# Two more attention scores a phase through VectorE and one exponential over 3072 columns

## The chip, the cores and the metric

The kernel runs on one core of a Trainium2 chip. The metric is the time of one execution on the device, in microseconds (us); smaller is better. Before the change three runs gave 1272.70, 1272.88 and 1272.94, so the median is 1272.88 us.

The engines are called as in the profile: PE is TensorE (PEld its weight loads), DVE is VectorE, ACT is ScalarE, POOL is GpSimd, and SP issues the DMAs.

## What is computed

The reference mixes two results for each of 2048 tokens of 512 channels: a full softmax attention with 32 heads of 16 channels, and a token-mixing MLP, weighted by a gate of each token.

```python
def reference(A_x, A_wqkv, A_wo, B_x, B_w1, B_b1, B_w2, B_b2, gate_w):
    x = A_x                                   # (1, 2048, 512)
    g = sigmoid((x * gate_w).sum(-1, keepdims=True))
    # a: qkv = x @ wqkv; 32 heads of 16; softmax(q k^T / 4) v; then @ wo
    # b: layernorm(x); gelu over tokens with w1 (2048x1792), b1; then w2, b2
    return g * a + (1 - g) * b
```

Everything is float32. For each head there are 2048 x 2048 scores, and every one goes through an exponential on ACT.

## The kernel before

**Stages.** Until about 278 us the kernel projects q, k and v and computes the first MLP layer. Then come 128 *phases* of attention, and at the end the output projection of the last tokens. The second MLP layer, the projections of late queries and those of the first half of the output run as *dense* matmuls inside the phases.

**A phase.** A group `grp` is two heads by 1024 queries; it has four phases (`ph` 0 to 3). A phase computes 16 scores, numbered `n` = 0 to 15, each a matmul into one PSUM bank of 128 x 512 (L1025). Heads take one half of PE's rows each, and a dense matmul (L1034) runs in the other half beside the first `n_b` scores; `n_b` is 14 in phases of the second layer and 12 in those of a projection. Scores get to exponentials by three roads:

- SINGLE, n = 0, 2, 4, 6, 8, 9: ACT reads the bank and writes `p1` (L1046, 128x512).
- TWO, pairs (10,11), (12,13), (14,15): ACT reads two adjacent banks at once and writes `p2` (L991, 128x1024). The helper is `exps(n)`.
- EVAC, n = 1, 3, 5, 7: DVE copies the bank to `pe` in SBUF (L1042), and at the phase's end ACT takes the exponential of all four in place (L1057, 128x2048).

Then PE multiplies the exponentials by v into the bank `av` (L921, the function `apply_v`), and DVE adds `av` to the sums `ot` (L943). What a phase cannot have in time is *held*: its EVAC units (`HELD`) and its last pair are multiplied at the start of the next phase's `apply_v`.

**PSUM.** Eight banks: one is `dn`, the accumulator of the dense matmuls, with one buffer; seven serve scores and `av`. Score 10 takes the bank of score 3, score 11 that of 4, and so on to 14 (bank of 7, which was first that of 0) and 15 (bank of 8); `av` takes that of 9. Each waits until DVE or ACT has read what was there. Score 6 of a phase takes the bank that `av` had in the phase before, and so waits for DVE's addition.

**Order.** The attention part stands under a manual schedule: each engine runs its instructions in the order of the Python code. On DVE a phase is: its copies, then what a finished dense row needs (`second_out` L542, `out` of a late query L604 to L611, `output` L791), a tiny memset `mark`, splits of weights (L67), jobs put there by `on_dve` (L1073), and the additions L943. The late query's `out` reads `dn` in its first three operations and in its last, the `TENSOR_REDUCE` of L611, and the first dense matmul of the next phase writes `dn` anew. There are eight late queries.

**A wait written by hand.** The exponential over the copies waits for DVE's copies; by L1058 it also waits for an ACT instruction, `pairs_done[1]`, the second pair's exponential of the phase. With that on record a later instruction needs to wait for one engine alone:

```python
tc.add_manual_dep(done.ins, pairs_done[1].ins.name, SYNC, reason=EARLY)
```

Of the kernel before, what the change touches and what calls it, by code (L numbers as in the profile page):

```python
# [9 lines left out]
F32 = mybir.dt.float32  # L10
# [13 lines left out]
P = 128  # L24
# [8 lines left out]
NB = 512  # L33
# [27 lines left out]
def gated_mix(ctx: ExitStack, tc: tile.TileContext, a_x, a_wqkv, a_wo, b_w1, b_b1, b_w2, b_b2, gate_w, out):  # L61
# [116 lines left out]
    with tc.tile_pool(name="vp", bufs=1, side="right") as pool:  # L178
# [15 lines left out]
        turns = {}  # L194
# [378 lines left out]
    LAST = NG * PHASES - 1  # L573
# [301 lines left out]

    token, mark = (out_pool.tile([1, 1], F32, name=name, bufs=1) for name in ("token", "mark"))

    EVAC = 1, 3, 5, 7
    SINGLE = 0, 2, 4, 6, 8, 9
    TWO = (10, 11), (12, 13), (14, 15)  # L880
    TURNS = [(0, 2), (4, 6), (8, 9), *TWO]
    HELD = [(1, 3), (5, 7)]

    def shares(n):

# [62 lines left out]
    with tc.manual_schedule(engines=engines):  # L948
        held, fence, turn, spare = [], None, 0, 0
        landed.clear()  # L950

        for p in range(LAST + 1):
            grp, ph = divmod(p, PHASES)
            second = ph % 2
            if ph == 0:
                sums[grp] = ot_pool.tile([P, NB], F32, name="ot")
                latest["clear"] = nc.gpsimd.memset(sums[grp], 0.0)
                at = [[0, 0], [0, 0]]
                if grp + 1 < NG:
                    qt[grp + 1] = load_q(grp + 1)  # L960
            if ph == 1 and grp + 1 < NG:
                kt[grp + 1] = load_k(grp + 1)
            for what, *args in calls.get(p, ()):
                what(*args)
            if not second:
                beside = [step(*args) for step, *args in dense.get(p // 2, ())]
            n_b = len(beside)
            half = slice(0, HALF) if second else slice(HALF, P)

            head = [second if n < n_b else (n - n_b + second * n_b) % 2 for n in range(NSC)]  # L970
            qbs = {}
            order = list(TURNS)
            if ph == 0 and n_b == NSC - 4:
                order[-2:] = (12, 14), (13, 15)
            for a, b in order + HELD:
                if head[a] == head[b]:
                    qbs[a], qbs[b] = 0, 1
                else:
                    zero, one = (a, b) if head[a] == 0 else (b, a)
                    qbs[zero], qbs[one] = turn, 1 - turn  # L980
                    turn = 1 - turn

            swap = ph == PHASES - 1 and p < LAST and n_b == NSC - 2
            if swap:
                order[-2:] = order[:-3:-1]

            def exps(n):
                pt = ptp.tile([P, 2, NB], F32, name="p2", bufs=len(TWO) + 1)
                where = [share[(j - BANKS) % BANKS] for j in (n - 1, n)]
                low = min(where)  # L990
                pairs_done.append(nc.scalar.activation(pt, twos[low, low + 1], AF.Exp, scale=SCALE))  # L991
                for j, k in zip((n - 1, n), where):
                    units[j] = *units[j][:3], pt[:, k - low, :]

            pairs_done = []
            evac = evp.tile([P, len(EVAC), NB], F32, name="pe")
            units = {}
            share = shares(spare)
            pool = regions()
            psum = pool.__enter__()  # L1000
            ones = [psum.tile([P, NB], F32, name=f"s{n}") for n in range(BANKS)]
            for n in range(NSC):
                i, qb = head[n], qbs[n]
                c = at[i][qb]
                at[i][qb] += 1
                if n < TWO[0][0]:
                    if n >= BANKS:
                        ones[share[n - BANKS]] = psum.tile([P, NB], F32, name=f"s{share[n - BANKS]}")
                    s = ones[share[n % BANKS]]
                else:  # L1010
                    if n == TWO[0][0]:
                        pool.__exit__(None, None, None)
                        pool = regions()
                        psum = pool.__enter__()
                        twos = {}
                        for low in range(BANKS):
                            if low == share[2]:
                                av = psum.tile([P, NB], F32, name="av")
                            elif low not in twos:
                                two = psum.tile([P, 2, NB], F32, name=f"t{low}")  # L1020
                                twos[low], twos[low + 1] = two[:, 0, :], two[:, 1, :]
                                twos[low, low + 1] = two
                    s = twos[share[(n - BANKS) % BANKS]]
                rows_i = slice(i * HALF, i * HALF + ROWS)
                nc.tensor.matmul(  # L1025
                    s,
                    kt[grp][rows_i, c * P : (c + 1) * P],
                    qt[grp][rows_i, qb * NB : (qb + 1) * NB],
                    start=True,
                    stop=True,  # L1030
                )
                if n < n_b:
                    ps, a, b, begin, last, done = beside[n]
                    mm = nc.tensor.matmul(ps, a[half], b[half], start=begin and not second, stop=last and bool(second))  # L1034
                    if n == 0 and fence is not None:
                        tc.add_manual_dep(mm.ins, fence.ins.name, SYNC, reason=REASON)
                    if n == n_b - 1:
                        fence = nc.gpsimd.memset(token, 0.0)  # L1038
                        tc.add_manual_dep(fence.ins, mm.ins.name, SYNC, reason=REASON)
                if n in EVAC:  # L1040
                    pt = evac[:, EVAC.index(n), :]
                    nc.vector.tensor_copy(pt, s)  # L1042
                    units[n] = i, c, qb, pt
                elif n in SINGLE:
                    pt = ptp.tile([P, NB], F32, name="p1", bufs=len(SINGLE))
                    nc.scalar.activation(pt, s, AF.Exp, scale=SCALE)  # L1046
                    units[n] = i, c, qb, pt
                else:
                    units[n] = i, c, qb, None
                    if n == TWO[0][1] or n == TWO[1][1] and not swap:  # L1050
                        exps(n)
                    elif n == TWO[2][1]:
                        exps(n)
                        if swap:
                            exps(TWO[1][1])
            for x in ([evac] if p < LAST else [evac[:, :2, :], evac[:, 2:, :]]):
                done = nc.scalar.activation(x, x, AF.Exp, scale=SCALE)  # L1057
            tc.add_manual_dep(done.ins, pairs_done[1].ins.name, SYNC, reason=EARLY)  # L1058
            evac_done.append(done)
            if n_b and second and beside[-1][-1]:  # L1060
                beside[-1][-1]()
            if p == 0:
                shift_rows(nc.gpsimd, k_bufs[1])
            if p:
                met = nc.vector.memset(mark, 0.0)
                for before in (evac_done[-2], latest["add"], latest["clear"]):
                    tc.add_manual_dep(met.ins, before.ins.name, SYNC, reason=EARLY)
            if second:
                for _ in range(2):
                    if len(ready) < 2:  # L1070
                        split_weight(nc.vector.tensor_copy)
            for what, *args in later.get(p, ()):
                what(*args)  # L1073

            turns, now_held = ([tuple(units[n] for n in pair) for pair in pairs] for pairs in (order, HELD))
            spare = share[2]
            if p < LAST:
                now_held = now_held + turns[-1:]
                turns = turns[:-1]
            if ph == 0:  # L1080
                if held:
                    apply_v(av, grp - 1, held, final=True)
                    spare = share[3]
                    av = twos[spare]
                apply_v(av, grp, turns)
            elif p < LAST:
                apply_v(av, grp, held + turns, await_loads=ph == PHASES - 1)
            else:
                ot = sums[grp]
                nc.vector.tensor_scalar_max(ot, ot, least[0])  # L1090
                apply_v(av, grp, held + turns + now_held, final=True)
                last_ot = ot
            pool.__exit__(None, None, None)
            held = now_held
            if ph == PHASES - 1:
                assert at == [[NS, NS], [NS, NS]]
# [166 lines left out]
```

## Time and profile before

| what | value |
|---|---|
| median of the runs | 1272.88 us |
| the profiled execution | 1273.23 us, of which the span of the profile is 1271.4 us |
| granted TensorE clock | 0.999 |
| PE / ACT / DVE / POOL busy over the span | 99% / 85% / 54% / 16% |
| L1046, six singles a phase | 768 exponentials |
| L991, three pairs a phase | 384 exponentials |
| L1057, one over the copies a phase | 129 exponentials (two in the last phase) |
| L1042, four copies a phase | 512 copies |

In the profile's rows of a timeline the columns are start (us from the span's start), duration (us), engine, line and operation, written tile and read tile with their shapes, and how many were merged in the row. A merged row runs from the start of its first instruction to the end of its last. Instructions of ACT overlap: the next one starts before the one ahead of it has ended, so the sum of durations is more than the time that they take.

### The profile page before, as it was taken

The numbers are of one execution on the slowest core, as the hardware profiler recorded it, in microseconds if no ns is written. First come the engines' busy times: TensorE is split into PE (matmuls) and PEld (weight loads), VectorE is DVE, ScalarE is ACT, GpSimd is POOL, SyncE is SP. The second block draws the span as 40 slices with busy tenths as digits, with TensorE's granted clock in tenths as the row PEclk, the third lists the DMA queues.
The fourth block names the chain that finished last, engine by engine and source line by source line (L and its number), as shares of the span: only waits on it lengthen the run. The fifth ranks groups of instructions, "written<-read, shape, count | busy, mean of one in ns | idle before, by whom it ended". The sixth has DMA issues, their size and how long they took to land.

```text
span 1271.4 us, 32690 instructions
## 1 busy us (share of the span) xinstructions
PE 1263.2 (99%) x13342; PEld 827.5 (65%) x13342; DVE 685.1 (54%) x1282; ACT 1076.4 (85%) x1533; POOL 198.9 (16%) x316
## 2 busy tenths in 40 slices
PE   9999999999999999999999999999999999999998
PEld 7888888875666666666566666666666666655556
DVE  5675453176645554555555455554555455456763
ACT  4443343269999999999999999999999999999990
POOL 0220444561011101010110101111111111000000
PEclk9999999999999999999999999999999999999999
DMA  3798443253654443534344443443543443366511
GB/s 132 247 343 328 139 128 100 79 133 114 206 124 102 86 104 77 163 79 97 80 99 101 92 100 74 90 86 77 116 101 63 98 100 60 56 167 184 140 57 70
DMA packets 100555, 152.32 MB, mean 120 GB/s; under 512 B 17109, under 2 KB 56171, under 8 KB 96300
## 3 DMA queue, kind: packets, MB, share of 16 engines
q1 hardware_dynamic: 99820, 149.08, 45.6%
q8 instruction: 108, 1.77, 0.6%
q10 hardware_dynamic: 576, 1.05, 0.2%
q14 instruction: 51, 0.42, 0.1%
HBM read 105.39 MB, written 44.68 MB: 118 GB/s over the span
## 4 chain that ended last, share of the span: by engine, by line
PE 93%; ACT 5%; DMA 0%; DVE 0%; issue 0%; SPq 0%
PE av L921 29%; PE s L1025 21%; PE acc L424 12%; PE t L1025 12%; PE acc L75 8%; PE t L921 5%; PE dn L1034 2%; ACT p L1046 2%; PE pa L1115 2%; ACT p L991 2%; ACT pe L1057 1%; PE acc L199 1%; PE acc L268 0%; DMA x<-in_A_x_dram 0%; PE pa L1145 0%
## 5 line engine op out<-in xcount | busy, mean ns | idle before, releaser
L1046 ACT ACTIVATE p<-s 128x512 f32<-128x512 f32 x768 | 421.8, 863 | 0.1
L991 ACT ACTIVATE p<-t 128x1024 f32<-128x1024 f32 x384 | 404.9, 1341 | 0.0
L1025 PE MATMUL s<-qs,ks 64*128 64x512 f32 x1280 | 329.7, 400 | 0.5 <-ACT p L1046 0.4
L1042 DVE COPY pe<-s 128x512 f32<-128x512 f32 x512 | 318.1, 684 | 4.8 <-PE s L1025 0.6
L921 PE MATMUL av<-p,v 128*32 128x256 f32 x4904 | 288.1, 379 | 0.0
L1025 PEld LDWEIGHTS s<-qs,ks 64*128 64x128 f32 x1280 | 226.1, 184 | 93.5 <-issue 51.9
L1057 ACT ACTIVATE pe<-pe 128x2048 f32<-128x2048 f32 x129 | 286.2, 2222 | 0.0
L943 DVE TENSOR_TENSOR ot<-av,ot 128x512 f32<-128x512 f32 (+2 forms) x140 | 84.8, 606 | 358.0 <-PE av L921 357.7
L921 PEld LDWEIGHTS av<-p,v 128*32 128x32 f32 x4904 | 159.4, 110 | 105.2 <-issue 0.2
L1025 PE MATMUL t<-qs,ks 64*128 64x512 f32 x768 | 189.4, 428 | 0.0
L1034 PE MATMUL dn<-u_hi,w_hi 64*128 64x512 f32 x448 | 182.4, 407 | 0.0
L1034 PE MATMUL dn<-u_lo,w_hi 64*128 64x512 f32 x448 | 182.2, 407 | 0.0
L1034 PE MATMUL dn<-u_hi,w_lo 64*128 64x512 f32 x448 | 182.2, 407 | 0.0
L68 POOL TENSOR_TENSOR w_lo<-w_raw,w_hi 128x512 fp32r<-128x512 f32 (+1 forms) x128 | 152.9, 1201 | 121.4 <-ACT w_hi L67 99.8
L1025 PEld LDWEIGHTS t<-qs,ks 64*128 64x128 f32 x768 | 96.3, 184 | 87.6 <-ACT p L1046 87.5
L1038 POOL MEMSET token<- 1x1 f32 x128 | 12.0, 94 | 829.5 <-PE dn L1034 776.8
L921 PE MATMUL av<-pe,v 128*32 128x256 f32 x2048 | 137.3, 385 | 0.1
L67 ACT CAST w_hi<-w_raw 128x512 fp32r<-128x512 f32 (+1 forms) x67 | 38.0, 570 | 82.7 <-PE acc L424 63.1
L921 PEld LDWEIGHTS av<-pe,v 128*32 128x32 f32 x2048 | 53.5, 109 | 60.9 <-ACT p L1046 38.4
L424 PE MATMUL acc<-h_hi,w_hi 128*128 128x512 f32 x224 | 87.9, 392 | 0.0
L424 PE MATMUL acc<-h_hi,w_lo 128*128 128x512 f32 x224 | 87.8, 392 | 0.0
L424 PE MATMUL acc<-h_lo,w_hi 128*128 128x512 f32 x224 | 87.8, 392 | 0.0
(161 smaller groups left out, 1446.4 us busy)
## 6 DMA issues: line engine op xcount, KB each, us to landing
w_raw<-in_B_w_dram SPq DMA_DIRECT2D x96, 256.0 KB
ks<-kp SPq DMA_DIRECT2D x192, 128.0 KB
qs<-qp SPq DMA_DIRECT2D x256, 64.0 KB
kp<-pc SPq DMA_DIRECT2D x16, 512.0 KB
qp<-pc SPq DMA_DIRECT2D x8, 768.0 KB
qp<-row SPq DMA_DIRECT2D x24, 256.0 KB
v<-v SPq DMA_DIRECT2D x4, 1088.0 KB
x<-in_A_x_dram SPq DMA_DIRECT2D x16, 256.0 KB
```

The costliest lines, as they stand in the source:

```text
L67: copy(hi, src)
L68: return sub(lo, src, hi.bitcast(F32), ALU.subtract)
L75: nc.tensor.matmul(ps, a, b, start=start and n == 0, stop=stop and n == last)
L424: nc.tensor.matmul(p, a, b, start=first and k == 0, stop=last and k == 2)
L921: mm = nc.tensor.matmul(av[32 * j : 32 * (j + 1), i * QC : (i + 1) * QC], vb[b][:, v_at : v_at + 32], pt[:, h * QC : (h + 1) * QC], start= ...
L943: latest["add"] = nc.vector.tensor_tensor(x, y, x, ALU.add)
L991: pairs_done.append(nc.scalar.activation(pt, twos[low, low + 1], AF.Exp, scale=SCALE))
L1025: nc.tensor.matmul(s, kt[grp][rows_i, c * P : (c + 1) * P], qt[grp][rows_i, qb * NB : (qb + 1) * NB], start=True, stop=True,)
L1034: mm = nc.tensor.matmul(ps, a[half], b[half], start=begin and not second, stop=last and bool(second))
L1042: nc.vector.tensor_copy(pt, s)
L1046: nc.scalar.activation(pt, s, AF.Exp, scale=SCALE)
L1057: done = nc.scalar.activation(x, x, AF.Exp, scale=SCALE)
```

## The change

Scores 14 and 15 leave the pairs and join the scores that DVE copies. So DVE makes six copies a phase, ACT has two pairs (10,11) and (12,13), and the exponential over the copies has 3072 columns. `HELD` gets the pair (14,15), so the same two scores are multiplied by v in the next phase as in most phases before. `p2` has two buffers instead of four, `pe` is 3072 wide instead of 2048. Three special orders of the pairs (`order[-2:]`, `swap`) are gone. The order in which PE computes the last scores is made by the list `in_turn`; with n_b = 12 it is 12, 14, 13, 15. The line of the wait by hand is as it was, but `pairs_done` now has two entries.

```diff
-    EVAC = 1, 3, 5, 7
+    EVAC = 1, 3, 5, 7, 14, 15
     SINGLE = 0, 2, 4, 6, 8, 9
-    TWO = (10, 11), (12, 13), (14, 15)
+    TWO = (10, 11), (12, 13)
     TURNS = [(0, 2), (4, 6), (8, 9), *TWO]
-    HELD = [(1, 3), (5, 7)]
+    HELD = [(1, 3), (5, 7), (14, 15)]
...
-            head = [second if n < n_b else (n - n_b + second * n_b) % 2 for n in range(NSC)]
+            alone = NSC - (NSC - n_b) // 2
+            head = [second if n < alone else 1 - second for n in range(NSC)]
+            in_turn = list(range(n_b)) + [n for pair in zip(range(n_b, alone), range(alone, NSC)) for n in pair]
             qbs = {}
-            order = list(TURNS)
-            if ph == 0 and n_b == NSC - 4:
-                order[-2:] = (12, 14), (13, 15)
-            for a, b in order + HELD:
+            for a, b in TURNS + HELD:
...
-            swap = ph == PHASES - 1 and p < LAST and n_b == NSC - 2
-            if swap:
-                order[-2:] = order[:-3:-1]
-
             def exps(n):
-                pt = ptp.tile([P, 2, NB], F32, name="p2", bufs=len(TWO) + 1)
+                pt = ptp.tile([P, 2, NB], F32, name="p2", bufs=len(TWO))
...
-            for n in range(NSC):
+            for n in in_turn:
...
-                    if n == TWO[0][1] or n == TWO[1][1] and not swap:
+                    if n in (TWO[0][1], TWO[1][1]):
                         exps(n)
-                    elif n == TWO[2][1]:
-                        exps(n)
-                        if swap:
-                            exps(TWO[1][1])
             for x in ([evac] if p < LAST else [evac[:, :2, :], evac[:, 2:, :]]):
                 done = nc.scalar.activation(x, x, AF.Exp, scale=SCALE)
             tc.add_manual_dep(done.ins, pairs_done[1].ins.name, SYNC, reason=EARLY)
...
-            turns, now_held = ([tuple(units[n] for n in pair) for pair in pairs] for pairs in (order, HELD))
+            turns, now_held = ([tuple(units[n] for n in pair) for pair in pairs] for pairs in (TURNS, HELD))
             spare = share[2]
-            if p < LAST:
-                now_held = now_held + turns[-1:]
-                turns = turns[:-1]
```

On ACT the end of a phase stood so before; `p` is the tile of singles (128x512) and pairs (128x1024), `pe` that of the copies, and the square brackets name the engines whose semaphores are waited for:

```order
L1046 ACTIVATE p_3413<-s_3410 128x512 [waits PE_49]
L991 ACTIVATE p_3428<-t_3422 128x1024 [waits PE_49]
L991 ACTIVATE p_3432<-t_3419 128x1024 [waits PE_49]
L991 ACTIVATE p_3436<-t_3421 128x1024 [waits PE_49]
L1057 ACTIVATE pe<-pe 128x2048 [waits DVE_49,Activation_49]
L1046 ACTIVATE p_3488<-s_3482 128x512 [waits PE_49]
```

And now:

```order
L1041 ACTIVATE p_3414<-s_3411 128x512 [waits PE_49]
L986 ACTIVATE p_3429<-t_3423 128x1024 [waits PE_49]
L986 ACTIVATE p_3435<-t_3420 128x1024 [waits PE_49]
L1048 ACTIVATE pe<-pe 128x3072 [waits DVE_49,Activation_49]
L1041 ACTIVATE p_3489<-s_3483 128x512 [waits PE_49]
```

The third pair is gone. The second pair, for which the exponential over the copies waits on ACT's own semaphore, stood two places ahead of it and now stands directly ahead.

On DVE a phase that ends a late query stood so before; `row` and `z` are what `out` writes, `dn` is the accumulator:

```order
L1042 COPY pe<-s_3511 128x512
L67 CAST row<-dn 128x512
L68 TENSOR_TENSOR row<-dn,row 128x512
L609 TENSOR_SCALAR row<-dn,most 128x512
L610 SCALAR_TENSOR_TENSOR row<-row 128x512
L611 TENSOR_REDUCE z<-dn 128x1
L1065 MEMSET mark 1x1
L943 TENSOR_TENSOR ot<-av,ot 128x512
```

And now:

```order
L1037 COPY pe<-s_3512 128x512
L1037 COPY pe<-t_3532 128x512 x2
L67 CAST row<-dn 128x512
L68 TENSOR_TENSOR row<-dn,row 128x512
L609 TENSOR_SCALAR row<-dn,most 128x512
L610 SCALAR_TENSOR_TENSOR row<-row 128x512
L611 TENSOR_REDUCE z<-dn 128x1
L1056 MEMSET mark 1x1
L943 TENSOR_TENSOR ot<-av,ot 128x512
```

The two copies of the last scores stand between the four early copies and all of DVE's other work of the phase.

## The prediction

> **What bounds the kernel now.** I read the page first, then ACT's timeline, then one phase on all engines.
>
> ```profile
> PE 1263.2 (99%) x13342; PEld 827.5 (65%) x13342; DVE 685.1 (54%) x1282; ACT 1076.4 (85%) x1533; POOL 198.9 (16%) x316
> PE 93%; ACT 5%; DMA 0%; DVE 0%; issue 0%; SPq 0%
> ```
>
> The busy shares and the chain both name PE. But PE's busy time is modelled, and the chain goes back along PE wherever its records touch. The question is who sets the length of a phase, and ACT's timeline tells it: an undisturbed phase, then a disturbed one, then the last.
>
> ```profile
> 711.49 2.25 ACT L1057 ACTIVATE pe<-pe 128x2048 f32<-128x2048 f32 x1
> 713.38 3.31 ACT L1046 ACTIVATE p<-s 128x512 f32<-128x512 f32 x6
> 716.26 3.17 ACT L991 ACTIVATE p<-t 128x1024 f32<-128x1024 f32 x3
> 718.97 2.25 ACT L1057 ACTIVATE pe<-pe 128x2048 f32<-128x2048 f32 x1
> ...
> 1187.48 3.17 ACT L991 ACTIVATE p<-t 128x1024 f32<-128x1024 f32 x3
> 1190.41 2.04 ACT L1057 ACTIVATE pe<-pe 128x2048 f32<-128x2048 f32 x1
> 1192.21 3.17 ACT L1046 ACTIVATE p<-s 128x512 f32<-128x512 f32 x6
> 1195.08 3.06 ACT L991 ACTIVATE p<-t 128x1024 f32<-128x1024 f32 x3
> 1197.79 2.13 ACT L1057 ACTIVATE pe<-pe 128x2048 f32<-128x2048 f32 x1
> ...
> 1232.38 3.15 ACT L991 ACTIVATE p<-t 128x1024 f32<-128x1024 f32 x3
> 1235.09 2.31 ACT L1057 ACTIVATE pe<-pe 128x1024 f32<-128x1024 f32 x2
> ```
>
> From 713.38 to 1192.21 lie 64 phases: 7.48 us each, whether 14 or 12 dense matmuls run beside. So PE's own work does not set the length. Read ends instead of starts. The exponential over the copies ends at 713.74, the sixth single at 716.69 (0.49 each), the third pair at 719.43 (0.91 each), the next one over copies at 721.22 (1.79). These sum to 7.48 with no gap. In the disturbed phase the start of L1057 slips by about 0.2, to 0.24 before the last pair ends (1190.65), and its end (1192.45) and the next (1199.92) still keep 7.48. So **ACT is saturated**, and it stays so because the next instruction has already started when one ends: a start that is a little late costs nothing as long as it comes before that end.
>
> How much earlier is needed is seen in the first phase, where ACT had been idle:
>
> ```profile
> 278.60 3.26 ACT L1046 ACTIVATE p<-s 128x512 f32<-128x512 f32 x6
> 281.70 2.90 ACT L991 ACTIVATE p<-t 128x1024 f32<-128x1024 f32 x3
> 284.42 1.99 ACT L1057 ACTIVATE pe<-pe 128x2048 f32<-128x2048 f32 x1
> 286.22 3.12 ACT L1046 ACTIVATE p<-s 128x512 f32<-128x512 f32 x6
> ```
>
> Starts follow each other by 0.48 for a single (716.26 - 713.38 over 6), 0.905 for a pair (284.42 - 281.70 over 3) and 1.80 after the 2048 columns. Without a queue a pair lasts 2.90 - 2 x 0.905 = 1.09 from start to end, so 0.18 of it lies under the next instruction; queued it lasts 1.36.
>
> **The change on ACT.** If saturation stays, ACT saves one instruction's fixed part. The last phase has 1024 columns from SBUF twice: from the pairs' end (1235.53) to 1237.40, 0.935 each. Another 1024 columns cost 1.79 - 0.935 = 0.855, so 3072 take 2.645 where a pair and 2048 took 0.91 + 1.79 = 2.70: 0.06 a phase, 7.6 us over 127 phases.
>
> But the exponential over the copies waits by hand for `pairs_done[1]`. Before, this was the second of three pairs; a third lay between, and it had ended (719.43 - 0.91 = 718.52) before L1057 started at 718.97, so the wait cost nothing. Now it is the pair directly ahead: **ACT must stand still from the end of that pair until its own semaphore has come back.** The trace before shows no ACT instruction that waits for the one ahead of it. The nearest row is DVE's own chain in the fence below: L67 ends at 454.97, and L68, which reads its result, starts at 455.01, 0.04 later. I take 0.04. Bounds: nothing at all (saturation stays, -0.06 a phase) and 0.15, several times the row.
>
> The new phase, from the first single's start: six singles 6 x 0.478 = 2.87; the first pair 0.905; the second pair, with no queue now, ends 1.08 after its start (a hundredth under the third's 1.09); wait 0.04; from the start of 3072 columns to the next start 1.80 + 0.85 = 2.65 (512 columns more are 0.905 - 0.478 = 0.427). Sum 7.545 against 7.48: **+0.065 a phase, 127 phases, +8.3 us**. By the bounds -7.6 to +22.
>
> The Trainium skill's page "ScalarE: Activation LUTs", section "What ACT_TABLE_LOAD costs", gives an ACTIVATE with immediate operands 186 ns + 0.833 ns a column, and an overlap of about 93 ns between two back to back. By it the stop would cost 0.09 + 0.04, an estimate of 7.42 + 0.13 = 7.55 a phase; its 1.04 for a pair is near the 1.09 of the first phase.
>
> **The change on DVE.** One phase with n_b = 14:
>
> ```profile
> 705.36 0.49 PE L1025 MATMUL s<-qs,ks 64*128 64x512 f32 x1
> 705.89 3.31 ACT L1046 ACTIVATE p<-s 128x512 f32<-128x512 f32 x6
> 706.12 2.48 DVE L1042 COPY pe<-s 128x512 f32<-128x512 f32 x4
> 708.84 0.42 PE L1025 MATMUL t<-qs,ks 64*128 64x512 f32 x2
> 709.25 1.07 PE L921 MATMUL av<-pe,v 128*32 128x256 f32 x16
> 712.98 0.69 DVE L943 TENSOR_TENSOR ot<-av,ot 128x512 f32<-128x512 f32 x1 [3.83 <-PE av L921]
> ```
>
> Copies follow each other by (2.48 - 0.69)/3 = 0.60. Scores 14 and 15 end at 709.26; their copies run from 709.29 to 710.58, while the second pair ends at about 711.03 (709.20 for the last single, plus 2 x 0.91). So the copies are in time by 0.4 and do not set L1057. The two copies themselves (2 x 0.60 x 128 phases = 154 us of DVE) are hidden in DVE's idle time. The price is that everything behind them starts about 4.43 after the first copy instead of 2.41, and must be done when the addition is due, 6.86 after it. This window of 2.4 to 2.5 us is enough for most phases, and not for two kinds.
>
> *Late queries, 8 phases.* Here `out` holds `dn`:
>
> ```profile
> 454.28 0.69 DVE L67 CAST row<-dn 128x512 fp32r<-128x512 f32 x1
> 455.01 0.69 DVE L68 TENSOR_TENSOR row<-dn,row 128x512 fp32r<-128x512 f32 x1
> 457.00 0.68 DVE L611 TENSOR_REDUCE z<-dn 128x1 f32<-128x512 f32 x1
> 458.54 0.50 PE L1025 MATMUL s<-qs,ks 64*128 64x512 f32 x1
> 458.55 0.50 PE L1034 MATMUL dn<-u_hi,w_hi 64*128 64x512 f32 x1
> 459.07 3.30 ACT L1046 ACTIVATE p<-s 128x512 f32<-128x512 f32 x6
> 459.11 0.39 PE L1025 MATMUL s<-qs,ks 64*128 64x512 f32 x1
> ```
>
> `out` starts some 1.9 later, so L611 ends at 459.6 instead of 457.68, and the dense matmul due at 458.55 waits 1.05 to 1.1. PE goes in order, so behind it wait scores 1, 2 and all others; score 2 comes at 460.2, ACT's second single can start at 460.6. With the longer phase ACT lags PE by some 0.35, and its second single was due at 459.07 + 0.35 + 0.48 = 459.9. Loss 0.7, **8 x 0.7 = +5.6 us** (bounds 0.5 and 1.0: 4 to 8).
>
> *Long jobs behind the copies, 6 phases*, from their first start to their last end:
>
> ```profile
> 917.97 0.42 DVE L67 CAST w_hi<-w_raw 128x512 fp32r<-128x512 f32 x1
> 920.46 0.69 DVE L1073 TENSOR_TENSOR v<-row,v 128x512 fp32r<-128x512 f32 x1
> ...
> 1037.64 0.42 DVE L67 CAST w_hi<-w_raw 128x512 fp32r<-128x512 f32 x1
> 1040.33 1.11 DVE L1073 TENSOR_TENSOR v<-row,v 128x512 fp32r<-128x512 f32 x1
> ...
> 1068.11 0.81 DVE L542 TENSOR_SCALAR row<-dn,b2x,omg 128x512 f32<-128x512 f32 x1 [0.48 <-PE t L1025]
> 1071.34 0.69 DVE L1073 TENSOR_TENSOR v<-row,v 128x512 fp32r<-128x512 f32 x1
> ...
> 1187.29 0.75 DVE L791 SCALAR_TENSOR_TENSOR row<-dn,g,row 128x512 f32<-128x512 f32 x1
> 1189.38 1.22 DVE L68 TENSOR_TENSOR v<-o_sum,v 128x1024 fp32r<-128x1024 f32 x1
> ```
>
> That is 3.2, 3.8, 3.9 and 3.3; two further phases are like the first two kinds (at 304 and 948). Over a window of 2.5 they are 0.7 to 1.4 late, and the addition and the next copies with them. Score 14 waits for the fourth copy with 0.17 to spare, the copies of 14 and 15 have 0.45 before ACT stops for them; what exceeds 0.6 is lost: 0.1, 0.7, 0.8, 0.2 and again 0.1 and 0.7. **+2.5 us** (bounds 0 and the whole lateness, 6).
>
> **PE and the end.** PE gets the same matmuls; with n_b = 12 score 13 is computed after 14, a slot later, still before ACT wants it. In the last phase four units instead of two are multiplied after the last exponential:
>
> ```profile
> 1237.45 0.64 PE av L921 x8
> ```
>
> Eight more records, 8 x 0.057 (64 records take 3.65), are +0.45, less 0.06: **+0.4 us**.
>
> **Sum**: 8.3 + 5.6 + 2.5 + 0.4 = +16.8. The span of 1271.4 becomes 1288.2; on the median of 1272.88, 0.35 under the profiled execution's 1273.23, this gives **1289.7 us**.
>
> **Rivals.**
>
> *The wait is dearer* (0.15 instead of 0.04): +14 more, 1303.7. For it: ACT has never been seen to wait on itself here. Against: hand-overs between engines are fast too (the last single ends at 709.20, PE starts on it at 709.25). Chance 0.10.
>
> *The wait is free, DVE's lateness remains*: -7.6 + 5.6 + 3.8 + 0.4 (in a saturated ACT the long jobs have 0.2 less to spare) = +2.2, 1275.1. It would need the semaphore some 0.1 before the recorded end. Chance 0.08.
>
> *Faster: one instruction's fixed cost saved.* Its place is L1057 on a saturated ACT, its price -0.06 a phase; it decides if ACT restarts without a gap and DVE's lateness stays inside the slack, at `dn` as well. Then -7.6 + 0.4 = -7.2, 1265.7. For it speak the ends without a gap; against it the wait, which is in the built order. Chance 0.04. In the Trainium skill, "Perfetto Trace Analysis", section "Optimizing Scalar/DVE Operations", this is a rule: grouping into larger operations can raise throughput if the engine is saturated; the trace bears out the fixed cost, not the absence of a new stop.
>
> *DVE's lateness passes on to further phases*: 16 instead of 8 us, 1297.7. Against it: the phases after are light. Chance 0.06.
>
> **How the numbers follow.** My forecast has 0.72, with a range of its own of 1283 to 1297 (wait 0.02 to 0.08, queries 4 to 7, jobs 1 to 4). For 8 in 10 the range must leave out the free wait and most of the dear one: 1280 to 1299. A difference of 0.2%, 2.5 us, is about what can be told from none. Faster 0.04; within 0.2% half of the free-wait case, 0.04; slower 0.92.
>
> **What would show it.** Right: the phase's pitch on ACT is 7.54 to 7.55 in light phases; the 3072-column exponential starts 0.03 to 0.05 after the second pair's end, not before it; pairs last about 1.07 instead of 1.36; in 8 places PE's first dense matmul waits for DVE L611 by about 1 us. Wrong: starts before the pair's end and a pitch of 7.42 (free wait); a pitch of 7.65 (dear wait); L1057 waiting for DVE instead of ACT.

## The result, and the profile after

The changed kernel takes 1428.61 us (median of 4 runs, 1427.88 to 1428.90); the kernel before, run beside it, 1272.91. The ratio is 1.122, with a 95% interval of 1.120 to 1.124. The profiled execution took 1428.9 us with a span of 1427.0, which is 155.6 more than before at the same granted clock (0.999). Slower was forecast, but by 17 us (1289.7, range 1280 to 1299).

The page of the changed kernel, engines, chain and the groups around the scores (busy time in us and mean duration in ns, then the idle time just before them in us and what ended most of it):

```profile
PE 1315.3 (92%) x13342; PEld 871.7 (61%) x13342; DVE 866.3 (61%) x1547; ACT 1098.9 (77%) x1405; POOL 198.8 (14%) x316
...
PE 89%; DVE 9%; issue 1%; ACT 0%; DVEq 0%
...
L1041 ACT ACTIVATE p<-s 128x512 f32<-128x512 f32 x768 | 391.5, 615 | 60.2 <-PE s L1020 45.2
L1048 ACT ACTIVATE pe<-pe 128x3072 f32<-128x3072 f32 x129 | 354.1, 2747 | 73.2 <-DVE mark L1056 45.7
L1020 PE MATMUL t<-qs,ks 64*128 64x512 f32 x768 | 248.1, 428 | 103.5 <-DVE pe L1037 99.3
...
L1037 DVE COPY pe<-t 128x512 f32<-128x512 f32 x256 | 177.0, 692 | 158.9 <-PE t L1020 158.9
```

The same groups on the page of before:

```profile
L1046 ACT ACTIVATE p<-s 128x512 f32<-128x512 f32 x768 | 421.8, 863 | 0.1
L1057 ACT ACTIVATE pe<-pe 128x2048 f32<-128x2048 f32 x129 | 286.2, 2222 | 0.0
L1025 PE MATMUL t<-qs,ks 64*128 64x512 f32 x768 | 189.4, 428 | 0.0
```

DVE has entered the chain with 9%, and ACT has gone from it. ACT, which had no gap in a phase before, now idles 60 us ahead of the singles and 73 us ahead of the exponential over the copies. (For most of the 73 us the page names DVE's tiny `mark`; in the phase below it ends together with the last copy, at 710.99.) The last two rows of the changed kernel are the telling ones. PE idles before matmuls into `t` and waits for a DVE copy; DVE idles before copies out of `t` and waits for a PE matmul. The view of waits says how often (total us, times, longest):

```profile
DVE pe L1037 <- PE t L1020: 158.9, 256, 0.7
PEld t L1020 <- DVE pe L1037: 139.5, 128, 1.1
...
PE t L1020 <- DVE pe L1037: 99.3, 128, 0.8
```

256 is two copies a phase; 128 is one matmul a phase. The timeline of one phase shows which one. It is of the same kind as the phase shown of before (from 705.36 there), with n_b = 14 and no late query, and stands eight phases earlier in the order:

```profile
708.51 0.47 PE L1020 MATMUL t<-qs,ks 64*128 64x512 f32 x1
708.52 2.00 ACT L986 ACTIVATE p<-t 128x1024 f32<-128x1024 f32 x2
...
709.01 0.69 DVE L1037 COPY pe<-t 128x512 f32<-128x512 f32 x1 [0.65 <-PE t L1020]
...
709.76 0.50 PE L1020 MATMUL t<-qs,ks 64*128 64x512 f32 x1 [0.78 <-DVE pe L1037]
...
710.19 1.50 PE L921 MATMUL av<-pe,v 128*32 128x256 f32 x24
710.30 0.69 DVE L1037 COPY pe<-t 128x512 f32<-128x512 f32 x1 [0.59 <-PE t L1020]
...
711.08 2.77 ACT L1048 ACTIVATE pe<-pe 128x3072 f32<-128x3072 f32 x1 [0.56 <-DVE pe L1037]
...
713.78 0.49 PE L1020 MATMUL s<-qs,ks 64*128 64x512 f32 x1
...
714.31 0.60 ACT L1041 ACTIVATE p<-s 128x512 f32<-128x512 f32 x1 [0.46 <-PE s L1020]
```

Score 14 is computed at 708.51. Score 15 does not run at once with it, as it did before, but waits until DVE has copied score 14 (709.01 to 709.70) and starts at 709.76. PE goes in order, so the multiplication by v starts 1.68 after score 14 (710.19); before, it was 0.41 (708.84 to 709.25, in the prediction's rows). That puts 1.27 us on PE's own path in each phase. The second pair ends at 710.52, the copy of score 15 only at 710.99, so the exponential over 3072 columns starts 0.56 after that pair's end. The next phase's first score comes when the multiplications are through, and ACT's first single waits 0.46 for it.

**The sum.** From 705.64 to 714.31, one phase's first single to the next, are 8.67 us (rows of ACT below, under the experiment that moves the wait). Over 127 phases, 1.19 more than 7.48 make 151 of the 155.6 us. The late queries lose 0.43 each on top (9.09 to 9.11 from start to start), 3.4 in all; a few phases with long DVE jobs lose up to 0.8.

**Why does score 15 wait?** The two scores lie in different banks, but in one tile: `t` is two banks wide, and its halves are handed out as `twos[low]` and `twos[low + 1]`:

```python
two = psum.tile([P, 2, NB], F32, name=f"t{low}")
twos[low], twos[low + 1] = two[:, 0, :], two[:, 1, :]
```

Before, one ACT instruction read both halves after both had been written. Now the code writes one half, reads it with DVE, then writes the other. The PSUM pools are opened with `reuse_waits="tile"`. Listed with its waits, the built program has this on PE, of which the rows shown ahead of the prediction, of ACT and DVE, tell nothing:

```
L1020 MATMUL t_9920<-qs,ks 128x512 [waits DVE_49,Activation_49]
L1020 MATMUL t_9920<-qs,ks 128x512 [waits DVE_49]
```

The first wait frees the banks of the round before. The second is the new one, and without the waits the two rows read as one, "x2". The wait is one that the program asks for. That the tile, and not the order of the instructions or DVE's load, makes it had still to be tested; no run opens the pools in another way.

### The profile page after: what moved, and what is told of

The parts are those of the page before. It is cut to its first block, busy times and chain, and to the rows that moved or that the text cites. A ratio compares the mean times of both kernels' runs of the same rounds, so it can differ in the third digit from the quotient of the medians.

```text
span 1427.0 us, 32783 instructions
## 1 busy us (share of the span) xinstructions
PE 1315.3 (92%) x13342; PEld 871.7 (61%) x13342; DVE 866.3 (61%) x1547; ACT 1098.9 (77%) x1405; POOL 198.8 (14%) x316
## 4 chain that ended last, share of the span: by engine, by line
PE 89%; DVE 9%; issue 1%; ACT 0%; DVEq 0%
PE av L921 25%; PE s L1020 17%; PE t L1020 14%; PE acc L424 11%; PE acc L75 7%; PE dn L1029 7%; DVE pe L1037 6%; PE t L921 5%; PE pa L1103 2%; PE acc L199 1%; PE acc L268 0%; DVE row L610 0%; DVE row L68 0%; DVE row L67 0%; DVE row L609 0%
## 5 line engine op out<-in xcount | busy, mean ns | idle before, releaser
L1041 ACT ACTIVATE p<-s 128x512 f32<-128x512 f32 x768 | 391.5, 615 | 60.2 <-PE s L1020 45.2
L1048 ACT ACTIVATE pe<-pe 128x3072 f32<-128x3072 f32 x129 | 354.1, 2747 | 73.2 <-DVE mark L1056 45.7
L1020 PE MATMUL t<-qs,ks 64*128 64x512 f32 x768 | 248.1, 428 | 103.5 <-DVE pe L1037 99.3
L1037 DVE COPY pe<-t 128x512 f32<-128x512 f32 x256 | 177.0, 692 | 158.9 <-PE t L1020 158.9
L986 ACT ACTIVATE p<-t 128x1024 f32<-128x1024 f32 x256 | 255.9, 1089 | 0.0
L1020 PEld LDWEIGHTS t<-qs,ks 64*128 64x128 f32 x768 | 128.9, 184 | 206.0 <-DVE pe L1037 139.5
L921 PE MATMUL av<-p,v 128*32 128x256 f32 x3880 | 227.2, 379 | 0.0
L921 PE MATMUL av<-pe,v 128*32 128x256 f32 x3072 | 192.3, 383 | 0.0
L921 PEld LDWEIGHTS av<-p,v 128*32 128x32 f32 x3880 | 126.1, 110 | 83.3 <-issue 0.2
L921 PEld LDWEIGHTS av<-pe,v 128*32 128x32 f32 x3072 | 86.9, 109 | 75.1 <-issue 30.0
```

The source lines that it names most:

```text
L921: mm = nc.tensor.matmul(av[32 * j : 32 * (j + 1), i * QC : (i + 1) * QC], vb[b][:, v_at : v_at + 32], pt[:, h * QC : (h + 1) * QC], start= ...
L1020: nc.tensor.matmul(s, kt[grp][rows_i, c * P : (c + 1) * P], qt[grp][rows_i, qb * NB : (qb + 1) * NB], start=True, stop=True,)
```

## Experiments: which wait sets the phase

**Both copies behind both scores** (e1). The copies of 14 and 15 are issued after both matmuls; tiles and everything else stay.

```diff
-                    nc.vector.tensor_copy(pt, s)
+                    if n < TWO[0][0]:
+                        nc.vector.tensor_copy(pt, s)
+                    else:
+                        late_copies.append((pt, s))
+                        if n == in_turn[-1]:
+                            for pair in late_copies:
+                                nc.vector.tensor_copy(*pair)
```

> The changed kernel, but DVE's copies of scores 14 and 15 both stand behind score 15. Theory: in the changed kernel score 15 waits until DVE has copied score 14, because both lie in one two-bank tile and the wait is kept by tile; a phase took 8.67 us there. Without that wait the phase falls to about 7.55 and the kernel to about 1290 us (1280 to 1299). Rival, the two copies themselves are too much for DVE: still above 1400 us, with the phase near 8.6.

Measured: 1295.14 us, ratio 1.0177 [1.0160, 1.0194]. 93 of 127 phases last 7.56.

**A bank and a tile for each** (e1b). The order of the change stays; only the two scores get tiles of one bank.

```diff
+                            elif low in share[:2]:
+                                twos[low] = psum.tile([P, NB], F32, name=f"u{low}")
```

> The changed kernel, but scores 14 and 15 get a tile of one bank each; nothing else moves, and the copy of 14 still stands ahead of score 15. Theory of the wait by tile: as fast as with both copies behind score 15, within 5 us, about 1288. Rival, it is the order of the instructions and not the tile: as slow as the changed kernel, about 1428.

Measured: 1290.27 us, ratio 1.0136 [1.0119, 1.0153]. DVE, then ACT, in a phase of it:

```profile
716.59 1.29 DVE L1039 COPY pe<-u 128x512 f32<-128x512 f32 x2 [0.59 <-PE u L1022]
```

```profile
716.29 1.99 ACT L986 ACTIVATE p<-t 128x1024 f32<-128x1024 f32 x2
718.31 2.77 ACT L1050 ACTIVATE pe<-pe 128x3072 f32<-128x3072 f32 x1
720.99 1.55 ACT L1043 ACTIVATE p<-s 128x512 f32<-128x512 f32 x3
```

The two copies now run one behind the other, 716.59 to 717.88, and are through 0.40 before the second pair ends (718.28): the 0.4 of the prediction. Two lines that change no order and no arithmetic take away 138 us. In the built program of e1b score 15 no longer waits for DVE. The edit also splits the wait for the banks of the round before between the two scores, but e1, which leaves the tile and takes away the write behind a read, saves 133 us without that. Both together show the cause: a write into one half of a tile waits for the reader of the other half.

**The tile's wait stays, the wait by hand moves to the first pair** (e7).

```diff
-            tc.add_manual_dep(done.ins, pairs_done[1].ins.name, SYNC, reason=EARLY)
+            tc.add_manual_dep(done.ins, pairs_done[0].ins.name, SYNC, reason=EARLY)
```

> The changed kernel with one edit: the exponential over the copies waits for the first pair instead of the second; the two-bank tile stays. Theory: while score 15 waits for the copy of score 14, PE sets the phase and ACT has idle time, so ACT's own wait costs nothing there: 1428, within 3 us, and the phase stays at 8.67. Rival, the two waits add up: some 15 us less, 1413.

Measured: 1428.07 us (2 runs), ratio 1.1218 [1.1197, 1.1238]. ACT before this edit (the changed kernel), and after it:

```profile
705.64 3.05 ACT L1041 ACTIVATE p<-s 128x512 f32<-128x512 f32 x6 [0.46 <-PE dn L1029]
708.52 2.00 ACT L986 ACTIVATE p<-t 128x1024 f32<-128x1024 f32 x2
711.08 2.77 ACT L1048 ACTIVATE pe<-pe 128x3072 f32<-128x3072 f32 x1 [0.56 <-DVE pe L1037]
```

```profile
705.18 3.05 ACT L1041 ACTIVATE p<-s 128x512 f32<-128x512 f32 x6 [0.47 <-PE dn L1029]
708.06 2.00 ACT L986 ACTIVATE p<-t 128x1024 f32<-128x1024 f32 x2
710.62 2.77 ACT L1048 ACTIVATE pe<-pe 128x3072 f32<-128x3072 f32 x1 [0.56 <-DVE pe L1037]
```

Not a hundredth has moved inside the phase. The wait of which the prediction made half its sum is worth nothing as long as DVE's copy ends later than the pair. Waits in parallel do not add up.

## Experiments: the terms of the forecast

**The wait by hand alone** (e2), in the kernel before:

```diff
-            tc.add_manual_dep(done.ins, pairs_done[1].ins.name, SYNC, reason=EARLY)
+            tc.add_manual_dep(done.ins, pairs_done[-1].ins.name, SYNC, reason=EARLY)
```

> The kernel before with one edit: the exponential over the copies waits for the last of the three pairs, which is directly ahead of it on ACT, instead of the second. Theory of the prediction: ACT stands still 0.12 to 0.13 us a phase, 7.48 becomes 7.60, +16 us, about 1289. Rival, the wait is free: 1273. Rival, the wait is dear (0.15 to come back instead of 0.04): above 1300.

Measured: 1290.73 us, ratio 1.0140 [1.0123, 1.0157]; 123 of 127 phases last 7.62. ACT:

```profile
713.65 3.02 ACT L1046 ACTIVATE p<-s 128x512 f32<-128x512 f32 x6
716.51 2.90 ACT L991 ACTIVATE p<-t 128x1024 f32<-128x1024 f32 x3
719.45 1.91 ACT L1057 ACTIVATE pe<-pe 128x2048 f32<-128x2048 f32 x1
721.26 1.07 ACT L1046 ACTIVATE p<-s 128x512 f32<-128x512 f32 x2
```

The third pair ends at 719.41, L1057 starts at 719.45. In the saturated phases of before, that exponential started 0.24 to 0.46 ahead of the pair's end. One wait on the instruction directly ahead costs 0.14 a phase, 18 us over 127 phases, with the same instructions on every engine.

**Without it** (e3: e1 and the wait on the first pair; e5: e1b and the same).

```diff
-            tc.add_manual_dep(done.ins, pairs_done[1].ins.name, SYNC, reason=EARLY)
+            tc.add_manual_dep(done.ins, pairs_done[0].ins.name, SYNC, reason=EARLY)
```

> Both copies behind score 15, and the exponential over the copies waits for the first of the two pairs instead of the second. Theory: ACT is saturated again with a phase of 7.42, so about 15 us less than with the wait on the second pair: 1270 to 1278, with DVE's late work in the 8 late queries and 6 long jobs still costing some 9 us. Rival, ACT's own wait costs nothing: the same as with both copies behind score 15 alone.

> Scores 14 and 15 in tiles of one bank each, and the exponential over the copies waits for the first pair instead of the second. Theory: both waits are gone, so phases with 14 and with 12 dense matmuls alike take 7.42 us (with both copies behind score 15 the latter took 7.62); DVE's late work stays, 8 late queries at about 0.6 to 1.0 us and some 6 long jobs. 1290.3 - 0.14 x 114 phases = 1274, within 1271 to 1278. Rival, ACT is not what sets the phase: no gain against own banks alone, 1290.

Measured: e3 1286.80, ratio 1.0113 [1.0096, 1.0130]; e5 1279.91, ratio 1.0054 [1.0040, 1.0068]. Phases with n_b = 14 that nothing delays last 7.42 in both, so the 0.06 of one exponential's fixed part are there once the wait is gone. Both miss the times expected of them, by three losses that the phases' lengths give: the late queries (8.2 in e5; 8.45 in e3, where both copies wait for score 15, which comes a slot later with n_b = 12), long jobs (up to 8.8, and 9.0 in e5's last phase but one), and all phases with n_b = 12: 7.62 in e3, 7.56 in e5. The last of these was new. A phase of e5 with n_b = 12, some rows of all engines:

```profile
1153.48 0.68 DVE L1039 COPY pe<-s 128x512 f32<-128x512 f32 x1
...
1154.21 0.18 PEld L1022 LDWEIGHTS u<-qs,ks 64*128 64x128 f32 x1 [0.35 <-DVE pe L1039]
1154.21 0.49 PE L1022 MATMUL u<-qs,ks 64*128 64x512 f32 x1
...
1154.22 0.50 PE L1022 MATMUL t<-qs,ks 64*128 64x512 f32 x1
...
1154.32 1.08 ACT L986 ACTIVATE p<-t 128x1024 f32<-128x1024 f32 x1
...
1154.55 0.39 PE L1022 MATMUL u<-qs,ks 64*128 64x512 f32 x1
...
1154.87 0.16 PEld L921 LDWEIGHTS av<-pe,v 128*32 128x32 f32 x8 [0.36 <-ACT p L1043]
```

The order 12, 14, 13, 15 puts score 14 (`u`) ahead of 13 (`t`). Score 14 takes the bank of score 7 and waits for that copy to end (1154.16); score 13, whose bank is free, waits behind it. The multiplication by v begins 0.55 after the first pair's start instead of 0.41 to 0.42, as in undisturbed phases with n_b = 14 of the same run. These 0.14 are what the phase loses (7.56 against 7.42). That the order is the reason was tested in e8.

**DVE's work spread out** (e6: e5 with five moves). The late query's cast stands ahead of copies 14 and 15 (`early`), and its last read of `dn` one operation earlier; two of the long jobs get later turns, and one an earlier turn:

```diff
-            nc.vector.scalar_tensor_tensor(most_k.bitcast(F32R), most_k, -1.0, most_k, ALU.mult, ALU.max)
             nc.vector.tensor_reduce(qmax[:, b, n : n + 1], ps, axis=AX.X, op=ALU.max, apply_absolute_value=True)
+            nc.vector.scalar_tensor_tensor(most_k.bitcast(F32R), most_k, -1.0, most_k, ALU.mult, ALU.max)
...
-        on_dve(at + 2, split, wq[0], wq[1], raw, nc.vector.tensor_copy, nc.vector.tensor_tensor)
+        on_dve(at + 7, split, wq[0], wq[1], raw, nc.vector.tensor_copy, nc.vector.tensor_tensor)
...
-        call(p0, fetch_left, k, p0 + 2, p0 + 2, p0 + 2)
+        call(p0, fetch_left, k, p0 + 2, p0 + 3, p0 + 3)
...
-    call(p0 + 9, fetch_o, 2, p0 + 11, p0 + 12, p0 + 12)
+    call(p0 + 9, fetch_o, 2, p0 + 10, p0 + 11, p0 + 11)
...
+                    if n == EVAC[-2] and n_b and second and hasattr(beside[-1][-1], "early"):
+                        beside[-1][-1].early()
```

> As the kernel with own banks and the earlier wait, and DVE's late work is moved: the first operation of a late query's output stands ahead of the copies of 14 and 15, its reduction ahead of the operation that does not read the accumulator, and the long jobs are spread over two phases. Theory: what is left above 7.42 us a phase is DVE's late work alone, so 127 phases of 7.42 give 1272.9 - 7.6 + 0.4 = 1266, within 1264 to 1269, faster than the kernel before. Rival, the late work is not what those phases wait for: the same as without the move, 1272 or more.

Measured: 1273.16 us over 11 runs, ratio 1.0004 [0.9995, 1.0013], no difference from the kernel before that can be told: 6.8 us less than e5, but outside the expected 1264 to 1269. The queries' stall is gone (7.36 a phase) and so are the long jobs' (7.41 to 7.42 where e5 had 8.6 to 8.7). The phases with n_b = 12 still last 7.56, and one phase lasts 12.77. DVE there:

```profile
1191.53 1.22 DVE L1076 TENSOR_TENSOR e<-o_sum,e 128x1024 fp32r<-128x1024 f32 x1
1191.55 0.06 DVE L1068 MEMSET mark<- 1x1 f32 x1
1197.90 1.23 DVE L1076 TENSOR_TENSOR o_sum<-v,o_sum 128x1024 f32<-128x1024 f32 x1 [5.14 <-DMA o_sum<-ri]
1199.04 0.68 DVE L951 TENSOR_TENSOR ot<-av,ot 128x512 f32<-128x512 f32 x1
```

The job with the earlier turn multiplies data of a DMA that has not landed. DVE goes in order, so the addition behind it, and with it a bank of PSUM, waits 5.1 us too.

**The order of scores as before, and that job late again** (e8).

```diff
-            head = [second if n < alone else 1 - second for n in range(NSC)]
-            in_turn = list(range(n_b)) + [n for pair in zip(range(n_b, alone), range(alone, NSC)) for n in pair]
+            head = [second if n < n_b else (n - n_b + second * n_b) % 2 for n in range(NSC)]
+            in_turn = list(range(NSC))
...
-    call(p0 + 9, fetch_o, 2, p0 + 10, p0 + 11, p0 + 11)
+    call(p0 + 9, fetch_o, 2, p0 + 11, p0 + 11, p0 + 12)
```

> As e6 (own banks for scores 14 and 15, the wait by hand on the first pair, DVE's work spread over more phases), but with n_b = 12 the scores are computed in the order of the kernel before (12, 13, 14, 15), and the third fetch of the last half's output has its multiplication one phase later again, where its data have arrived, with one of its three jobs and no longer two in the phase after. Theory (the order 12, 14, 13, 15 costs PE a slot in each of some 30 phases with n_b = 12, and the 5.3 us of e6 at phase 123 were a wait for a DMA that came too early in DVE's order): these phases fall from 7.555 to 7.42, no phase above 8 us is left but the two or three at the start, and 127 phases of 7.42 with some 2 to 3 us of early losses give 1263 to 1268 us, which is faster than before by 0.4 to 0.8%. Rival (these phases are bound by PE's matmul work with either order, since 16 copies' worth of banks come free too late): they stay at 7.55, only the 5.3 us are saved, and the time is 1267 to 1269 us, with ACT idle at the first exponential over the copies of each such phase.

Measured: 1267.40 us (1267.04 to 1267.78, 5 runs) against 1272.82, ratio 0.9956 [0.9943, 0.9970]: 5.4 us, or 0.4%, less than the kernel before, with an interval that leaves out 1, and 161 us less than the changed one. A phase with n_b = 12 on ACT, and the first row of the one after it:

```profile
392.19 3.24 ACT L1053 ACTIVATE p<-s 128x512 f32<-128x512 f32 x6
395.07 2.20 ACT L994 ACTIVATE p<-t 128x1024 f32<-128x1024 f32 x2
396.88 3.04 ACT L1060 ACTIVATE pe<-pe 128x3072 f32<-128x3072 f32 x1
399.61 3.25 ACT L1053 ACTIVATE p<-s 128x512 f32<-128x512 f32 x6
```

392.19 to 399.61 are 7.42, and the next instruction starts ahead of each end again: 397.27 is the second pair's end, 396.88 the start behind it. The time alone does not decide, since 1267.4 lies in the range of the rival too; the phases do, and the rival is out: ahead of the last 15 phases none with n_b = 12 lasts more than 7.43. Of 127 phases, 94 last 7.42 (within 0.01) in e8, 57 in e6. Four of the last 15 still last 7.65 to 7.96. In the kernel before the same four places show on ACT alone (7.61 to 7.62, made up in the phases behind), while PE keeps 7.48; what delays PE there in e8 stays open.

## Why the prediction was wrong

**The step that failed** is on DVE: "Scores 14 and 15 end at 709.26; their copies run from 709.29 to 710.58 … So the copies are in time by 0.4 and do not set L1057." It takes the end of both scores from a row of before (708.84, two matmuls merged, 0.42) that holds only because nobody read one of them before the other was written. "PE gets the same matmuls" counts PE's instructions and not their waits. In the changed kernel the scores are 1.25 apart, the second copy ends at 710.99 instead of 710.58, and, which weighs more, PE's multiplications start 1.27 later in each phase. What the runs show in its place (e1, e1b) is that score 15 waits for the copy of score 14, since both lie in one tile; this wait stood in no term of the sum. None of the rivals had it. The dearest of them was the dear wait on ACT, with 1303.7; no bound asked what PE may come to wait for.

**What was noted as a sign of error came**: L1048 waits for DVE and not for ACT.

**The bound.** "ACT is saturated" was right for before and wrong for after. PE's path, 8.67 less the new 1.27, is 7.40, and phases of e8 that catch up after a loss last 7.32 to 7.34. So PE lay only about 0.08 to 0.16 under ACT's 7.48, and whatever is put on PE's order beyond that shows in the time. This is an estimate from kernels whose PE order differs a little: in the kernel before, the first scores of 121 of 127 phases follow each other by the same 7.48 as ACT's singles, so PE's own pace cannot be read there. The prediction used "PE's own work does not set the length" without asking by how little.

**The other terms**, read where the tile's wait is gone (e1b). It takes 1290.27 where the prediction had 1289.7, and that is in part luck: the queries cost 2.0 less than forecast, the phases about 1 more, and a place that the prediction did not count 1.9 more.

| step of the prediction | forecast | measured |
|---|---|---|
| phase with the wait by hand | 7.545 | 7.56 |
| start of the exponential over the copies after the second pair's end | 0.04 | 0.03 |
| two pairs from start to end | 0.905 + 1.08 | 1.99 |
| the phase without that wait | 7.42 | 7.42 (e5, e8) |
| a late query, beyond its phase | 0.7 (0.5 to 1.0) | 0.43 to 0.51, 3.6 in all |
| long jobs, all together | 2.5 (its six terms add up to 2.6) | 2.4 in e1b at four places, and 1.9 at a fifth |

The wait's mechanism was right. The Trainium skill's page "ScalarE: Activation LUTs", section "What ACT_TABLE_LOAD costs", with its overlap of 93 ns between instructions back to back, gave an estimate of 7.55; e1b shows 7.56 and agrees.

The query's stall was mis-sized by score 2, for which ACT's second single waits. The dense matmul was 1.01 late, nearly as forecast. But score 1 ran beside it (461.98) and not behind it, so score 2 came 1.36 after score 0, not 1.66:

```profile
460.95 0.50 PE L1022 MATMUL s<-qs,ks 64*128 64x512 f32 x1
...
461.14 0.68 DVE L611 TENSOR_REDUCE z<-dn 128x1 f32<-128x512 f32 x1
...
461.97 0.46 PE L1031 MATMUL dn<-u_hi,w_hi 64*128 64x512 f32 x1 [0.53 <-DVE mark L1058]
...
461.98 0.49 PE L1022 MATMUL s<-qs,ks 64*128 64x512 f32 x1
...
462.31 0.39 PE L1022 MATMUL s<-qs,ks 64*128 64x512 f32 x1
...
462.74 2.56 ACT L1043 ACTIVATE p<-s 128x512 f32<-128x512 f32 x5 [0.32 <-PE s L1022]
```

(The rows are of e1b, of PE, DVE and ACT.) The long jobs were right in size where they delay copies (0.72 to 0.77 beyond a phase), and a place was missed, in the last phase but one: DVE waits for the load of `inv`, 3.26 in e1b and 2.75 in e5, and the addition behind it waits too. The trace of before has that wait as well, where it only just fitted, since the addition behind it, at 1221.60, still waited 0.15 for PE. The first row is of before, the second of e5, where that phase lasts 9.0 us:

```profile
1220.67 0.19 DVE L734 TENSOR_SCALAR inv<-inv 96x64 f32<-96x64 f32 x1 [2.71 <-DMA inv<-r]
...
1227.98 0.19 DVE L734 TENSOR_SCALAR inv<-inv 96x64 f32<-96x64 f32 x1 [2.75 <-DMA inv<-r]
```

In e8, where one job less stands ahead of the additions of the phase before, the load is issued 3.5 after the first copy of its phase instead of 4.9 in e5, and DVE does not wait for it. It also lands sooner after its issue, within 1.7 us instead of 2.9; why is open.

"A slot later, still before ACT wants it" for n_b = 12 was wrong as well; it costs 0.14 in each of 28 phases of e5 and was hidden in the changed kernel, whose phases last 8.67 with either n_b.

**What the faster rival lacked.** It named its mechanism, one exponential's fixed part less, and its two conditions, a restart without a gap and DVE's work inside the slack. Both can be made true (e8: 1267.4, where it gave 1265.7), but the change as written meets neither, and breaks a third that it did not name, two scores written before either is read. "Perfetto Trace Analysis", section "Optimizing Scalar/DVE Operations", of the Trainium skill, with its rule on grouping on a saturated engine, asks that the engine be saturated. Where it is (e8), the trace agrees, 7.42 against 7.48; in the changed kernel ACT was no longer saturated, and there was nothing to gain.

## What to carry to other kernels

When a reader moves to another engine or splits in two, look at each *tile* that it reads: a write to one part of it may now stand behind the reader of another part. Compare what each instruction waits for before and after, on every engine, PE too, and never in a list that folds equal rows. And for the engine that is just under the bound, write down by how much, since a new wait on it may take no more than that before the time grows.

## What the runs showed of the hardware

- A hand-over and back between PE and DVE costs little beside the copy: the score ends at 708.98, the copy starts at 709.01, ends at 709.70, and the next matmul starts at 709.76. Of the 1.25 us, 0.69 are the copy and 0.47 the matmul.
- ACT's wait for its own last instruction takes 0.03 to 0.04 us from end to start. What costs is that nothing is queued behind it: the pair that lasts 1.36 when queued lasts 1.08, and the phase still loses 0.14.
- A PE that is busy 92% of the span by the page waits for DVE in each of 128 phases. The share fell from 99% while its busy time rose from 1263 to 1315 us.
